# One bank for the picks' sums, three products of the features on GpSimd, and steps spread in issue order

## The chip, the cores and the metric

The program runs on one core of a Trainium2 chip. The metric is the device time of one execution in microseconds. Three executions of the kernel before took 787.77, 784.3 and 783.0 us, median 784.3. All data is float32 in memory.

## The reference

Three parts in a row. The first is a linear attention with a complex decay over 768 positions, 4 batches, 8 heads, 48 channels a head (q, k, v, a_re and a_im have the shape 4 x 8 x 768 x 48):

```
mag = sqrt(a_re^2 + a_im^2); scale = min(mag, 0.999) / (mag + 1e-6)
for t in range(768):
    (S_re, S_im) = (a_re, a_im)[t] * scale[t] * (S_re, S_im)      # complex product, per channel d
    S_re += outer(k[t], v[t])
    y[t] = q[t] @ S_re
```

Its output, 3072 tokens of 384 channels, goes through a mixture of 8 experts, one per token, chosen by an argmax (tokens with `x @ w_skip <= 0` pass unchanged): `x + gate * relu(x @ w1[e]) @ w2[e]`, with a gate from a softmax. The last part is `max(x @ m1, x @ m2, x @ m3) @ mo` with 768 inner channels.

## The kernel before

Attention runs first, the rest is a second plan that starts when its tokens are there. The recurrence is made parallel: running sums over time of the logarithm and of the angle of a turn it into products of features, and these into matrix products over chunks of 128 positions.

**Features.** A batch has three groups of 128 channel rows (`G = 3`; group g = 2 holds the channels 32 to 47 of all heads). For each group, tiles of 128 x 768: a_re and a_im (`a`), q and k (`qk`, 128 x 2 x 768), two work tiles (`CD`), and the result `R`. `ratio` (L338) takes Ln and Exp of a_re on ScalarE and multiplies by a_im on VectorE (L347), which is the ratio of the two. `stage_e` (L349) squares it on ScalarE (L352), takes more logarithms and exponentials, and scans the decay along time on VectorE (`decay`, L371). `scale` (L376) makes the reciprocal exact and multiplies `qk` with `CD` (L385, 128 x 1536). `stage_t` (L387) takes the arctangent, scans the angle (`phase`, L417), reduces it to a turn, takes sines, and makes the features by two products of 128 x 1536 (L406, L407: `R` and `qk`). `tails` copies group 2's features into the tile Y by DMAs on the SP queue. All VectorE work of a feature goes through the helper `V_` (L328; its instructions show as L332), all ScalarE work through `A_` (L300). A batch is a unit; the last batch has its group 1 cut in two parts of 4 and 2 chunks.

**Steps.** For each batch, each half of the heads (hh = 0, 1) and each chunk c of 128 positions, `step` (L459) does: transposes of k into the bank pk (L471), copied to kn by ScalarE (L473); scores of 4 heads into the 4 banks of pp (L482), copied by ScalarE to pt (L485) and masked there by GpSimd (L486; the last three steps by VectorE, L490; `POOL_MASKS` = 45 of 48); products of q with the state so far into py (L499); the state's sum z in its bank (L506), masked by VectorE into sn (L511); products of the masked scores with v into py (L519), copied by ScalarE to ysb (L521); the picks' product with w9p (L526), whose sums px lie in the upper part of py's own two banks; from there ScalarE copies the tokens to xt (L530), VectorE the router's sums to lgw (L532), and SP stores xt (L543). A step of chunk c needs the state of chunk c - 1 of its half. Banks: pk 1, pp 4, py 2, z 1: all eight. pk, pp and py exist once; pt and kn twice.

**Order.** Nothing is issued in the order written. `Plan` collects instructions with an engine, a guessed duration and the data they read and write, plays them through on these guesses (`order`), and issues each engine's instructions in the order of the planned starts. Of those that are ready it takes the one written first, shifted by a bias (`PRIO`, per batch). Each engine then runs its own list in that order on the chip and waits for data by semaphores; the guesses themselves have no further effect. Guesses are for example `t_act(n) = 93 + 0.833 n` ns for n columns on ScalarE; a rule for two-input work on GpSimd, `t_ptt(n) = 40 + 2.09 n`, stands in the file without use.

Of the kernel before, what the change touches and what calls it, by code (L numbers as in the profile page):

```python
# [166 lines left out]
NQK = 6  # L167
NR = 5
RHO0 = 2.0 ** 60
NA = 6  # L170
NPT = 2
XW = 2 * D + 9
# [13 lines left out]
def attention(tc, ctx, pl, a4, qk4, v, w9, x_dram, lg, ident, phend, rhoend, keep, early=None):  # L186
# [140 lines left out]

    def V_(name, out, *ins, n=None, bias=0, **kw):  # L328
        fn = getattr(nc.vector, name)
        t = (t_dcp if name == "tensor_scalar" else t_dve)(out[0].free_size() if n is None else n)  # L330
        names = ("in0", "in1")[:len(ins)]
        pl.add("DVE", t, lambda: fn(out=out[0], **{m: i[0] for m, i in zip(names, ins)}, **kw),  # L332
               keys(*ins), keys(out), bias=bias)

    def cut(t, n):
        return t[0][:, 0:n], t[1]

    def ratio(us):  # L338

        for u in us:  # L340
            t, k = place("CD", u)
            T[u, "C"], T[u, "D"], T[u, "CD"] = (t[:, 0, :], k), (t[:, 1, :], second(k)), (t, k + second(k))
        for w in runs(us, ("a",), "ratio"):
            A = many(w, "ar")
            A_(AF.Ln, many(w, "C"), A)
            A_(AF.Exp, A, many(w, "C"), scale=-1.0)
            V_("tensor_tensor", A, A, many(w, "ai"), op=ALU.mult, bias=PRIO["FE"][now[0]])  # L347

    def stage_e(us):  # L349
        for w in runs(us, ("a",), "log"):  # L350
            A, Dt = many(w, "ar"), many(w, "D")
            A_(AF.Square, Dt, A)  # L352
            A_(AF.Ln, Dt, Dt, bias=1.0)
        for w in runs(us, ("CD",), "size"):
            Ct, Dt = many(w, "C"), many(w, "D")
            V_("scalar_tensor_tensor", Ct, Ct, Dt, scalar=2.0, op0=ALU.mult, op1=ALU.add, bias=PRIO["FE"][now[0]])
            A_(AF.Exp, Dt, Ct, scale=0.5)
            V_("tensor_scalar", Dt, Dt, scalar1=0.999, scalar2=-1e-6, op0=ALU.min, op1=ALU.add, bias=PRIO["FE"][now[0]])
            for u in w:
                decay(u)  # L360
        for w in runs(us, ("CD",), "inv"):
            Ct, Dt = many(w, "C"), many(w, "D")
            A_(AF.Ln, Dt, Ct)
            A_(AF.Exp, Dt, Dt, scale=-1.0)

    def decay(u):
        b, g, c0, c1 = u
        Ct, Dt, i, n = T[u, "C"], T[u, "D"], b * G + g, C * (c1 - c0)

# [4 lines left out]
        pl.add("DVE", t_dve(n) + 200, scan, keys(Dt) + (("rho", i),), keys(Ct) + (("rho", i),), bias=PRIO["FE"][now[0]])  # L374
# [12 lines left out]
    def stage_t(us):  # L387
# [10 lines left out]
        for w in runs(us, ("a",), "trig"):  # L398
            A, Bt = many(w, "ar"), many(w, "ai")
            A_(AF.Abs, A, Bt)  # L400
            A_(AF.Sin, A, A, scale=-TWOPI_DOWN, bias=halfpi)
# [10 lines left out]
    def phase(u):  # L412
# [7 lines left out]
        pl.add("DVE", t_dve(n) + 200, scan, keys(A) + (("ph", i),), keys(Bt) + (("ph", i),), bias=PRIO["FT"][now[0]])  # L420

# [33 lines left out]

    prev = {}
    kfe = lambda fs: sum((f[1] for f in fs), ())

    def step(b, hh, c):  # L459
# [16 lines left out]
        pt, ptk = pl.take("pt")  # L476

        def f():
            for x, (t, _) in enumerate(fs):
                for h in range(4):  # L480
                    r = slice(ND * h, ND * h + ND)
                    nc.tensor.matmul(pp[:, h, 0:C], t[r, 1, :], t[r, 0, :], start=x == 0, stop=x == 2)  # L482
        pl.add("PE", 12 * 70, f, fk, (ppk,))
        if (2 * b + hh) * NC + c < POOL_MASKS:
            pl.add("ACT", t_acp(512), lambda: nc.scalar.copy(pt, pp[:, :, 0:C]), (ppk,), (ptk,), bias=PRIO["pt"][b])  # L485
            pl.add("POOL", 594, lambda: nc.gpsimd.affine_select(  # L486
                out=pt, in_=pt, pattern=[[0, 4], [1, C]], base=0, channel_multiplier=-1, compare_op=ALU.is_ge,
                fill=0.0), (ptk,), (ptk,))
        else:
            pl.add("DVE", t_dve(512), lambda: nc.vector.tensor_tensor(  # L490
                out=pt, in0=pp[:, :, 0:C], in1=mask[:, None, :].to_broadcast([P, 4, C]), op=ALU.mult), (ppk,), (ptk,), bias=PRIO["mask"][b])
        sp = prev.get((b, hh)) if c else None
        py, pyk = pl.take("py")
        if c:
            def f():
                for x, (t, _) in enumerate(fs):
                    for j in range(2):
                        r = slice(64 * j, 64 * j + 64)
                        nc.tensor.matmul(py[:, j, 0:C], sp[0][r, x].rearrange("p o w -> p (o w)"), t[r, 0, :], start=x == 0,  # L499
                                         stop=False, skip_group_check=True)  # L500
# [19 lines left out]
        pl.add("PE", 4 * 116, f, (vk, ptk) + ((pyk,) if c else ()), (("y", pyk),) if c else (("y", pyk), pyk))  # L520
        pl.add("ACT", t_acp(256) + 90, lambda: nc.scalar.copy(ysb, py[:, :, 0:C]), (("y", pyk), pyk), (ysk,), bias=PRIO["ysb"][b])  # L521
# [25 lines left out]
    def steps(us):  # L547
# [5 lines left out]
        for k, (b, hh) in enumerate((b, hh) for b in range(B) for hh in range(2)):  # L553
# [854 lines left out]
```

## Time and profile before

| | us |
|---|---|
| median of three executions | 784.3 |
| the profiled execution | 787.75 |
| its span | 786.0 |
| busy in the span: TensorE (PE) | 661.3 |
| VectorE (DVE) | 504.6 |
| ScalarE (ACT) | 373.2 |
| GpSimd (POOL) | 106.1 |

The profiled execution is one of its own, outside the three, and 3.45 us above their median. PE and PEld are TensorE's products and its weight loads. The span in 40 equal slices of 19.65 us; each digit is the busy share of a slice in tenths, in PEclk the granted clock in tenths of full speed:

```profile
PE   0037785877899884799999999999999999999996
DVE  6999889888751128599999975564736538313321
ACT  7597876776534323477777741232423224121221
POOL 2012012221111100211110016301202000000000
PEclk9998788597889998799999999999999999999998
```

Attention is the first 15 slices, to about 304 us; then come some 15 us of routing and first weights, and experts and the last part from 320 us on.

### The profile page before, as it was taken

What the parts mean: (1) busy time and instruction counts of PE and PEld (TensorE: products, weight loads), DVE (VectorE), ACT (ScalarE), POOL (GpSimd) and SP (SyncE); (2) the same over time, 40 slices, a digit from 0 to 9 for tenths busy, and PEclk for the clock granted to TensorE, in tenths of its full rate; (3) what the DMA queues carried; (4) which work ended last, traced back from release to release, by engine and by line L of the source; (5) the groups of instructions that cost most, each with busy time, mean ns of one, the idle gap of its engine ahead of it and who ended that gap; (6) DMA issues with size and microseconds to landing.
All of it is one profiled execution on the core that took longest, in us unless ns stands there. A gap on an engine that the chain in (4) does not pass through costs nothing.

```text
span 786.0 us, 14781 instructions
## 1 busy us (share of the span) xinstructions
PE 661.3 (84%) x5977; PEld 578.3 (74%) x5977; DVE 504.6 (64%) x828; ACT 373.2 (47%) x671; POOL 106.1 (13%) x151
## 2 busy tenths in 40 slices
PE   0037785877899884799999999999999999999996
PEld 0025664665677662699999989889789898898896
DVE  6999889888751128599999975564736538313321
ACT  7597876776534323477777741232423224121221
POOL 2012012221111100211110016301202000000000
PEclk9998788597889998799999999999999999999998
DMA  9661075411441003888888735514306031010000
GB/s 344 258 141 55 26 189 195 73 62 43 137 80 33 24 30 97 308 274 289 292 280 281 240 128 161 176 46 151 91 1 218 3 116 66 1 40 1 11 31 25
DMA packets 52108, 98.57 MB, mean 125 GB/s; under 512 B 5280, under 2 KB 41392, under 8 KB 52032
## 3 DMA queue, kind: packets, MB, share of 16 engines
q1 hardware_dynamic: 43408, 65.70, 26.8%
q10 hardware_dynamic: 5184, 20.45, 7.3%
q0 software_dynamic: 3440, 11.41, 4.8%
q8 instruction: 49, 0.80, 0.4%
q14 instruction: 27, 0.22, 0.1%
HBM read 80.23 MB, written 12.58 MB: 118 GB/s over the span
## 4 chain that ended last, share of the span: by engine, by line
PE 62%; DVE 17%; DMA 8%; issue 6%; ACT 4%; SPq 1%; POOL 0%; ACTq 0%; DVEq 0%; POOLq 0%
PE bk L838 10%; PE bk L839 10%; PE bk L840 10%; PE yb L840 5%; PE yb L839 5%; PE yb L838 5%; PE py L499 4%; PE pp L482 4%; PE py L526 3%; PE py L519 3%; DVE wa L417 2%; DMA x<-x_dram 2%; DMA wa<-in_a 2%; DVE wqk L332 2%; DVE wCD L371 2%
## 5 line engine op out<-in xcount | busy, mean ns | idle before, releaser
L838 PE MATMUL bk<-ar,wh 128*128 128x512 f32 (+1 forms) x378 | 136.4, 361 | 2.6 <-DVE xs L1117 2.0
L839 PE MATMUL bk<-ar,wh 128*128 128x512 f32 (+1 forms) x378 | 136.0, 360 | 0.1
L840 PE MATMUL bk<-ar,wl 128*128 128x512 f32 (+1 forms) x378 | 135.9, 360 | 0.0
L1117 DVE TENSOR_TENSOR xs<-bk,xs 128x512 f32<-128x512 f32 (+1 forms) x84 | 51.5, 613 | 90.8 <-PE bk L840 90.3
L838 PEld LDWEIGHTS bk<-ar,wh 128*128 128x128 f32 x378 | 71.4, 189 | 14.6 <-DVE xs L1117 3.0
L839 PEld LDWEIGHTS bk<-ar,wh 128*128 128x128 f32 x378 | 71.4, 189 | 10.6 <-DVE ar L1097 0.3
L840 PEld LDWEIGHTS bk<-ar,wl 128*128 128x128 f32 x378 | 71.4, 189 | 10.5
L486 POOL TENSOR_SCALAR_AFFINE_SELECT pt<-pt 128x512 f32<-128x512 f32 x45 | 44.5, 990 | 233.8 <-ACT pt L485 230.6
L834 DVE TENSOR_TENSOR ar<-wraw,ar 128x768 fp32r<-128x768 f32 x64 | 60.1, 953 | 5.8 <-ACT ar L833 5.2
L833 ACT CAST ar<-wraw 128x768 fp32r<-128x768 f32 x64 | 53.3, 835 | 15.1 <-PE yb L840 9.8
L838 PE MATMUL bk<-xth,ar 128*128 128x256 f32 x192 | 55.9, 291 | 1.2 <-DVE sm L935 0.7
L839 PE MATMUL bk<-xtl,ar 128*128 128x256 f32 x192 | 55.1, 287 | 0.1
L840 PE MATMUL bk<-xth,ar 128*128 128x256 f32 x192 | 54.9, 286 | 0.0
L471 PE MATMUL pk<-ident,wR 128*128 128x128 f32 x40 | 13.9, 347 | 48.7 <-DVE wR L332 48.1
L1119 ACT CAST sm<-xs 128x512 fp32r<-128x512 f32 (+1 forms) x27 | 15.1, 559 | 68.3 <-DVE xs L1117 68.3
L471 PEld LDWEIGHTS pk<-ident,wR 128*128 128x128 f32 x40 | 6.3, 157 | 53.9 <-issue 51.3
L838 PE MATMUL yb<-ar,sm 128*128 128x384 f32 x128 | 43.8, 342 | 0.0
L840 PE MATMUL yb<-ar,sm 128*128 128x384 f32 x128 | 43.1, 337 | 0.0
L839 PE MATMUL yb<-ar,sm 128*128 128x384 f32 x128 | 43.0, 336 | 0.0
L532 DVE COPY lgw<-py 128x18 f32<-128x18 f32 x48 | 8.3, 173 | 53.3 <-ACT xt L530 44.1
L300 ACT ACTIVATE wCD<-wCD 128x768 f32<-128x768 f32 (+3 forms) x51 | 39.5, 809 | 4.7 <-DVE wCD L371 4.2
L526 PE MATMUL py<-w9p,ysb 128*128 128x105 f32 x192 | 37.0, 321 | 4.7 <-ACT ysb L521 4.6
(232 smaller groups left out, 1604.0 us busy)
## 6 DMA issues: line engine op xcount, KB each, us to landing
wraw<-in_w SPq DMA_DIRECT2D x60, 384.0 KB, 4.8
wraw<-in_a ACTq DMA_DIRECT2D x12, 768.0 KB, 4.6
wqk<-in_qk SPq DMA_DIRECT2D x11, 768.0 KB, 9.0
x<-in_m ACTq DMA_DIRECT2D x9, 768.0 KB, 6.2
wa<-in_a SPq DMA_DIRECT2D x8, 768.0 KB, 5.8
v<-in_v SPq DMA_DIRECT2D x4, 1152.0 KB, 10.5
x_dram<-xt SPq DMA_DIRECT2D x48, 96.0 KB, 1.6
out<-ysb SPq DMA_DIRECT2D x24, 192.0 KB, 2.3
```

Source lines behind the costliest of these rows:

```text
L300: lambda: nc.scalar.activation(out=out[0], in_=in_[0], func=f, **kw), keys(in_), keys(out))
L482: nc.tensor.matmul(pp[:, h, 0:C], t[r, 1, :], t[r, 0, :], start=x == 0, stop=x == 2)
L486: pl.add("POOL", 594, lambda: nc.gpsimd.affine_select(out=pt, in_=pt, pattern=[[0, 4], [1, C]], base=0, channel_multiplier=-1, compare_op= ...
L499: nc.tensor.matmul(py[:, j, 0:C], sp[0][r, x].rearrange("p o w -> p (o w)"), t[r, 0, :], start=x == 0, stop=False, skip_group_check=True)
L519: nc.tensor.matmul(py[64 * o:64 * o + 64, j, 0:C], vcols(h), pt[:, h, :], start=not c, stop=True, skip_group_check=True)
L526: nc.tensor.matmul(px[:, j, :], ysb[:, j, :], w9p[:, 2 * hh + j, :], start=True, stop=True)
L833: pl.add("ACT", t_act(n), lambda: s.copy(hi, raw), r, wk_hi)
L834: pl.add("DVE", t_dve(n), lambda: v.tensor_tensor(out=lo, in0=raw, in1=f32(hi), op=ALU.subtract), tuple(r) + tuple(wk_hi), wk_lo)
L838: nc.tensor.matmul(ps, lh, rh, start=first, stop=False)
L839: nc.tensor.matmul(ps, lh, rl, start=False, stop=False)
L840: nc.tensor.matmul(ps, ll, rh, start=False, stop=last)
L1117: pl.add("DVE", t_dve(N), lambda tm=tm, ph=ph, N=N: v.tensor_tensor(out=tm[:, 0:N], in0=ph[:, 0:N], in1=tm[:, 0:N], op=ALU.max), (pk,) + t ...
```

## The change

The planner's guesses are set anew (ScalarE activations and copies, VectorE, a scan, TensorE's groups, the mask on GpSimd: 1000 ns), and `POOL_MASKS` is 48, so that all masks are GpSimd's. The picks' sums px get a bank of their own; for it pk goes, and the three transposes of k are written to columns 128 to 255 of three of the score banks, in the same group of TensorE work as the scores. kn is copied from there, and pt and kn have three buffers each. Three products of each group run on GpSimd: the ratio (128 x 768), the square (128 x 768, before ScalarE's) and qk with CD (128 x 1536). `pace` adds to the planner's list, for a batch but the last, a predecessor on VectorE for the k-th of its 12 score groups, such that the groups are spread over 95% of the planned VectorE work from this batch's first step to the next one's. These predecessors are used by the planner alone.

```diff
-t_act = lambda n: 93 + 0.833 * n
-t_acp = lambda n: 51 + 0.833 * n
-t_dve = lambda n: 70 + 1.04 * n
+t_act = lambda n: 150 + 0.85 * n
+t_acp = lambda n: 160 + 0.833 * n
+t_dve = lambda n: 90 + 1.04 * n
+t_scan = lambda n: 330 + 2.15 * n
-POOL_MASKS = 45
+POOL_MASKS = 48
+PACE = 0.95
+SIDE = {(w, b, g) for w in ("ratio", "scale", "square") for b in range(B) for g in range(G)}
-NPT = 2
+NPT = 3
-    ring("kn", [P, 3, P], 2)
+    ring("kn", [P, 3, P], 3)
-    ring("pk", [P, 512], 1, psum)
+    ring("px", [P, 512], 1, psum)
+    work = set()
...
-    def V_(name, out, *ins, n=None, bias=0, **kw):
-        fn = getattr(nc.vector, name)
+    def V_(name, out, *ins, bias=0, eng="DVE", **kw):
+        fn = getattr(nc.gpsimd if eng == "POOL" else nc.vector, name)
...
+        if eng == "DVE":
+            work.add(len(pl.ops))
+    def side(what, u):
+
+        return "POOL" if (what, u[0], u[1]) in SIDE else "DVE"
...
-            V_("tensor_tensor", A, A, many(w, "ai"), op=ALU.mult, bias=PRIO["FE"][now[0]])
+            V_("tensor_tensor", A, A, many(w, "ai"), op=ALU.mult, bias=PRIO["FE"][now[0]], eng=side("ratio", w[0]))
...
-            A_(AF.Square, Dt, A)
+            if side("square", w[0]) == "POOL":
+                V_("tensor_tensor", Dt, A, A, op=ALU.mult, eng="POOL")
+            else:
+                A_(AF.Square, Dt, A)
...
-                V_("tensor_tensor", T[u, "qk"], T[u, "qk"], T[u, "CD"], op=ALU.mult, bias=PRIO["scale"][now[0]])
+                V_("tensor_tensor", T[u, "qk"], T[u, "qk"], T[u, "CD"], op=ALU.mult, bias=PRIO["scale"][now[0]], eng=side("scale", u))
...
-        if not last:
-            pk, pkk = pl.take("pk")
-            kn, knk = pl.take("kn")
-
-            def f():
-                for x, (t, _) in enumerate(fs):
-                    nc.tensor.transpose(pk[:, x * P:x * P + P], t[:, 1, :], ident)
-            pl.add("PE", 3 * 97, f, fk, (pkk,))
-            pl.add("ACT", t_acp(384), lambda: nc.scalar.copy(kn.rearrange("p x r -> p (x r)"), pk[:, 0:3 * P]), (pkk,), (knk,),
-                   bias=PRIO["kn"][b])
...
-        pl.add("PE", 12 * 70, f, fk, (ppk,))
+            if not last:
+                for x, (t, _) in enumerate(fs):
+                    nc.tensor.transpose(pp[:, 1 + x, C:C + P], t[:, 1, :], ident)
+        gates_.setdefault(b, []).append(pl.add("PE", 880 if last else 1220, f, fk, (ppk,)))
...
+        if not last:
+            kn, knk = pl.take("kn")
+            pl.add("ACT", t_acp(384), lambda: nc.scalar.copy(kn, pp[:, 1:4, C:C + P]), (ppk,), (knk,), bias=PRIO["kn"][b])
...
-        px = py[:, :, C:C + XW]
+        px, pxk = pl.take("px")
+        px = px[:, 0:2 * XW].rearrange("p (j w) -> p j w", j=2)
...
-        pl.add("PE", 2 * 218, f, (ysk, "w9p"), (("px", pyk),))
+        pl.add("PE", 2 * 218, f, (ysk, "w9p"), (pxk,))
...
+            ends.setdefault(b, len(pl.ops))
             step(b, hh, c)
+
+    def pace():
+
+        dve = [i for i, o in enumerate(pl.ops) if o[0] == "DVE" and i in work]
+        for b in range(B - 1):
+            span = [i for i in dve if ends[b] <= i < ends[b + 1]]
+            total = sum(pl.ops[i][1] for i in span)
+            at, k = 0, 0
+            for i in span:
+                while k < len(gates_[b]) and at >= total * PACE * k / len(gates_[b]):
+                    if k and at:
+                        pl.ops[gates_[b][k]][3].setdefault(last_, False)
+                    k += 1
+                at += pl.ops[i][1]
+                last_ = i
```

## Rows read from the trace of the kernel before

**Rows 1.** Busy times by stretch: us, then PE, PEld, DVE, ACT, POOL, clock, DMA.
```profile
55.00:216.00 161.00, 122.34 (x1862) 95.79 (x1854) 137.92 (x181) 113.45 (x204) 32.42 (x28) 0.80 0.35 100
226.50:304.00 77.50, 68.59 (x1263) 53.99 (x1263) 20.51 (x62) 26.95 (x69) 10.15 (x16) 1.00 0.12 31
```

**Rows 2.** Timeline of VectorE, its ends: start us, us, instruction, [idle before].
```profile
225.78 0.68 DVE L332 TENSOR_TENSOR wqk<-wqk,wa 128x512 f32<-128x512 f32 x1
...
303.64 0.18 DVE L532 COPY lgw<-py 128x18 f32<-128x18 f32 x1
```

**Rows 3.** Groups by line of VectorE, 55 to 216 us: count, busy, mean ns, idle.
```profile
L511 DVE TENSOR_TENSOR sn<-zst,odd 128x288 f32<-128x288 f32 x24 | 10.9, 453 | 7.9 <-PE py L499 7.9
...
L532 DVE COPY lgw<-py 128x18 f32<-128x18 f32 x25 | 4.2, 170 | 13.2 <-PE py L526 9.0 <-ACT xt L530 4.2
```

**Rows 4.** Timeline of TensorE, products with v in the tail.
```profile
246.78 0.66 PE L519 MATMUL py<-pt,v 128*64 128x128 f32 x8
...
250.61 0.66 PE L519 MATMUL py<-pt,v 128*64 128x128 f32 x8
...
257.40 0.66 PE L519 MATMUL py<-pt,v 128*64 128x128 f32 x8
...
301.43 0.66 PE L519 MATMUL py<-pt,v 128*64 128x128 f32 x8
```

**Rows 5.** Timeline of VectorE, undisturbed: 768 and 1536 columns.
```profile
24.78 0.95 DVE L332 SCALAR_TENSOR_TENSOR wR<-wCD 128x768 f32<-128x768 f32 x1
25.65 1.75 DVE L332 TENSOR_TENSOR wqk<-wqk,wCD 128x1536 f32<-128x1536 f32 x1
```

**Rows 6.** Selects on GpSimd beside no features: a group, and one in the timeline.
```profile
L237 POOL TENSOR_SCALAR_AFFINE_SELECT mask<-mask 128x128 f32<-128x128 f32 x1 | 0.3, 292 | 0.0
...
244.59 0.63 POOL L486 TENSOR_SCALAR_AFFINE_SELECT pt<-pt 128x512 f32<-128x512 f32 x1 [2.86 <-ACT pt L485]
```

**Rows 7.** Timelines of VectorE and GpSimd, where a select meets a feature.
```profile
129.74 1.75 DVE L417 TENSOR_TENSOR_SCAN wa<-wa,zero 128x768 f32<-128x768 f32 x1
129.84 2.08 POOL L486 TENSOR_SCALAR_AFFINE_SELECT pt<-pt 128x512 f32<-128x512 f32 x1 [4.86 <-ACT pt L485]
...
181.29 0.63 POOL L486 TENSOR_SCALAR_AFFINE_SELECT pt<-pt 128x512 f32<-128x512 f32 x1 [6.06 <-ACT pt L485]
181.31 1.15 DVE L332 SCALAR_TENSOR_TENSOR wR<-wCD 128x512 f32<-128x512 f32 x1
182.50 0.69 DVE L332 SCALAR_TENSOR_TENSOR wCD<-wR,wCD 128x512 f32<-128x512 f32 x1
```

**Rows 8.** Groups by line: 1536-wide products without selects (20 to 55), with them, and selects.
```profile
L332 DVE TENSOR_TENSOR wR<-wqk,wa 128x1536 f32<-128x1536 f32 x3 | 5.3, 1751 | 0.0
L332 DVE TENSOR_TENSOR wqk<-wqk,wCD 128x1536 f32<-128x1536 f32 x3 | 5.3, 1750 | 0.0
L332 DVE TENSOR_TENSOR wqk<-wqk,wa 128x1536 f32<-128x1536 f32 x2 | 3.5, 1751 | 0.0
...
L332 DVE TENSOR_TENSOR wR<-wqk,wa 128x1536 f32<-128x1536 f32 x8 | 14.8, 1848 | 0.0
L332 DVE TENSOR_TENSOR wqk<-wqk,wCD 128x1536 f32<-128x1536 f32 x8 | 14.6, 1829 | 0.0
L332 DVE TENSOR_TENSOR wqk<-wqk,wa 128x1536 f32<-128x1536 f32 x8 | 14.3, 1788 | 0.0
...
L486 POOL TENSOR_SCALAR_AFFINE_SELECT pt<-pt 128x512 f32<-128x512 f32 x28 | 33.8, 1206 | 176.5 <-ACT pt L485 176.5
```

**Rows 9.** Groups by line of attention, 0 to 304 us: idle before, and releasers.
```profile
L482 PE MATMUL pp<-wR 32*128 32x128 f32 x384 | 27.3, 358 | 8.5 <-ACT pt L485 8.3
...
L499 PE MATMUL py<-wR,sn 64*128 64x128 f32 x160 | 22.8, 367 | 15.7 <-DVE lgw L532 12.4 <-ACT xt L530 3.3
...
L473 ACT COPY kn<-pk 128x384 f32<-128x384 f32 x40 | 19.3, 482 | 5.7 <-PE pk L471 2.7 <-PE zst L506 2.3
```

**Rows 10.** Timeline of the SP queue: four stores of a step.
```profile
74.46 21.12 SPq L543 DMA_DIRECT2D x_dram<-xt  x4
```

More of the change, by code (lines that the diff above doesn't have):

```diff
@@ L326, in keys @@
         return sum((t[1] for t in ts), ())
-    def V_(name, out, *ins, n=None, bias=0, **kw):
-        fn = getattr(nc.vector, name)
-        t = (t_dcp if name == "tensor_scalar" else t_dve)(out[0].free_size() if n is None else n)
+    def V_(name, out, *ins, bias=0, eng="DVE", **kw):
+        fn = getattr(nc.gpsimd if eng == "POOL" else nc.vector, name)
+        t = ((t_pts if name == "tensor_scalar" else t_ptt) if eng == "POOL" else t_dcp if name == "tensor_scalar" else t_dve)(out[0].free_size())
         names = ("in0", "in1")[:len(ins)]
-        pl.add("DVE", t, lambda: fn(out=out[0], **{m: i[0] for m, i in zip(names, ins)}, **kw),
+        if eng == "DVE":
+            work.add(len(pl.ops))
+        pl.add(eng, t, lambda: fn(out=out[0], **{m: i[0] for m, i in zip(names, ins)}, **kw),
                keys(*ins), keys(out), bias=bias)
@@ L373, in scan @@
             nc.vector.tensor_copy(out=rhoend[:, i:i + 1], in_=Ct[0][:, n - 1:n])
-        pl.add("DVE", t_dve(n) + 200, scan, keys(Dt) + (("rho", i),), keys(Ct) + (("rho", i),), bias=PRIO["FE"][now[0]])
+        work.add(len(pl.ops))
+        pl.add("DVE", t_scan(n), scan, keys(Dt) + (("rho", i),), keys(Ct) + (("rho", i),), bias=PRIO["FE"][now[0]])
     def scale(us):
@@ L399, in stage_t @@
             A, Bt = many(w, "ar"), many(w, "ai")
-            A_(AF.Abs, A, Bt)
+            if side("abs", w[0]) == "POOL":
+                V_("scalar_tensor_tensor", A, Bt, Bt, scalar=-1.0, op0=ALU.mult, op1=ALU.max, eng="POOL")
+            else:
+                A_(AF.Abs, A, Bt)
             A_(AF.Sin, A, A, scale=-TWOPI_DOWN, bias=halfpi)
@@ L419, in scan @@
             nc.vector.tensor_copy(out=phend[:, i, c0:c1], in_=c3(Bt[0])[:, :, C - 1])
-        pl.add("DVE", t_dve(n) + 200, scan, keys(A) + (("ph", i),), keys(Bt) + (("ph", i),), bias=PRIO["FT"][now[0]])
+        work.add(len(pl.ops))
+        pl.add("DVE", t_scan(n), scan, keys(A) + (("ph", i),), keys(Bt) + (("ph", i),), bias=PRIO["FT"][now[0]])
     def tails(u):
@@ L454, in feats @@
         return out
-    prev = {}
+    prev, gates_, ends = {}, {}, {}
     kfe = lambda fs: sum((f[1] for f in fs), ())
@@ L482, in f @@
                     nc.tensor.matmul(pp[:, h, 0:C], t[r, 1, :], t[r, 0, :], start=x == 0, stop=x == 2)
-        pl.add("PE", 12 * 70, f, fk, (ppk,))
+            if not last:
+                for x, (t, _) in enumerate(fs):
+                    nc.tensor.transpose(pp[:, 1 + x, C:C + P], t[:, 1, :], ident)
+        gates_.setdefault(b, []).append(pl.add("PE", 880 if last else 1220, f, fk, (ppk,)))
         if (2 * b + hh) * NC + c < POOL_MASKS:
             pl.add("ACT", t_acp(512), lambda: nc.scalar.copy(pt, pp[:, :, 0:C]), (ppk,), (ptk,), bias=PRIO["pt"][b])
-            pl.add("POOL", 594, lambda: nc.gpsimd.affine_select(
+            pl.add("POOL", 1000, lambda: nc.gpsimd.affine_select(
                 out=pt, in_=pt, pattern=[[0, 4], [1, C]], base=0, channel_multiplier=-1, compare_op=ALU.is_ge,
@@ L500, in f @@
                                          stop=False, skip_group_check=True)
-            pl.add("PE", 6 * 130, f, fk + (sp[1],), (pyk,))
+            pl.add("PE", 870, f, fk + (sp[1],), (pyk,))
         if not last:
@@ L507, in f @@
                                          start=c == 0 and x == 0, stop=c == NC - 2 and x == 2, skip_group_check=True)
-            pl.add("PE", 12 * 37, f, (vk, knk), ("z",) + (("begun",) if (b, hh, c) == (B - 1, 1, 0) else ()))
+            pl.add("PE", 390, f, (vk, knk), ("z",) + (("begun",) if (b, hh, c) == (B - 1, 1, 0) else ()))
             sn, snk = pl.take("sn")
@@ L520, in step @@
         pl.add("PE", 4 * 116, f, (vk, ptk) + ((pyk,) if c else ()), (("y", pyk),) if c else (("y", pyk), pyk))
-        pl.add("ACT", t_acp(256) + 90, lambda: nc.scalar.copy(ysb, py[:, :, 0:C]), (("y", pyk), pyk), (ysk,), bias=PRIO["ysb"][b])
-        px = py[:, :, C:C + XW]
+        pl.add("ACT", t_acp(256), lambda: nc.scalar.copy(ysb, py[:, :, 0:C]), (("y", pyk), pyk), (ysk,), bias=PRIO["ysb"][b])
+        px, pxk = pl.take("px")
+        px = px[:, 0:2 * XW].rearrange("p (j w) -> p j w", j=2)
         def f():
@@ L526, in f @@
                 nc.tensor.matmul(px[:, j, :], ysb[:, j, :], w9p[:, 2 * hh + j, :], start=True, stop=True)
-        pl.add("PE", 2 * 218, f, (ysk, "w9p"), (("px", pyk),))
+        pl.add("PE", 2 * 218, f, (ysk, "w9p"), (pxk,))
         xt, xtk = pl.take("xt")
         t0 = (b * NC + c) * C
-        pl.add("ACT", t_acp(192) + 90, lambda: nc.scalar.copy(xt.rearrange("p (j o) e -> p j (o e)", o=2), px[:, :, 0:2 * D]),
-               (("px", pyk), pyk), (xtk,), bias=PRIO["xt"][b])
+        pl.add("ACT", t_acp(192), lambda: nc.scalar.copy(xt.rearrange("p (j o) e -> p j (o e)", o=2), px[:, :, 0:2 * D]),
+               (pxk,), (xtk,), bias=PRIO["xt"][b])
         pl.add("DVE", 150, lambda: nc.vector.tensor_copy(out=lgw[:, (b * NC + c) % (2 * NC), 2 * hh:2 * hh + 2, :],
                                                          in_=px[:, :, 2 * D:]),
-               (("px", pyk), pyk), (("lgw", b % 2, c, hh),), bias=PRIO["lgw"][b])
+               (pxk,), (("lgw", b % 2, c, hh),), bias=PRIO["lgw"][b])
         sums = {NC - 1: 0} if b < B - 1 else {NC - 1 - LAST: 0, NC - 1: NC - LAST}
@@ L576, in attention @@
             stage_t(us)
+    pace()
     if early:
```

## The prediction

> **What bounds the kernel now.** I looked first at busy times by stretch, because a mean over the span mixes an attention stage with an expert stage that the change does not touch. From 55 to 216 us [rows 1] VectorE is busy 138 of 161 us while TensorE is busy 122 at a granted clock of 0.80; from 226.5 to 304 us VectorE is busy 21 of 77.5, and TensorE 69 at 1.00. So one stretch belongs to VectorE, the next to TensorE. Then the instructions in order of time [rows 2]: the last feature instruction of the last batch ends on VectorE at 226.5, the last instruction of the last attention step at 303.8. Call these F and E. Behind E come routing and experts, which wait for attention; I take them as shifted and otherwise unchanged. The change is worth what it moves E.
>
> Why 77 us between F and E? The groups by line [rows 3] count 25 finished steps by 216; two more end by F. So 21 of 48 steps are left: the 12 of the last batch, which could hardly come earlier, and 9 of the batch before, which could. The reader should see a backlog here: TensorE had been able to make a step only every 161/25 = 6.4 us while the features ran, against 3.83 us once they are gone (two successive products with v, [rows 4]). Twelve steps cost 11 x 3.83 from the first such product to the last, and 2.4 from there to the end [rows 2, 4], 44.5 us; in this kernel the same twelve took 46.4.
>
> **The change, part by part.**
>
> *Products to GpSimd: VectorE's relief.* Per group of features one 768-wide and one 1536-wide product leave VectorE. From start to start such instructions take 0.87 and 1.67 us [rows 5] (the printed time is 0.08 longer, an overlap). Twelve groups: 12 x 2.54 = 30.5 us. ScalarE loses a square per group; it is busy 113 of 161 us [rows 1], not the bound, so I count nothing for that.
>
> *The price on GpSimd.* No product of two tiles runs there before. The nearest rows are selects: 0.29 us for 128 columns, 0.63 for 512 [rows 6], so 0.9 ns a column and 0.18 fixed. Lower end: a product costs like a select, 0.86 and 1.54 us, 2 x 0.86 + 1.54 = 3.3 per group, 39 in all. Upper end: each of its two inputs costs what the select's one does, 1.55 and 2.92, 6.0 per group, 72 in all. I take the upper one, since two tiles have to be read. The Trainium skill, page "GPSIMD Engine Reference", section "Elementwise — side-by-side cycle accounting", measures 4497 ns for 2048 columns; as an estimate from that page 1.7 and 3.4 us, 81 in all, and the sum below would end 5 us later. No run here shows it.
>
> *What these 72 us take back from VectorE.* The rows show the engines holding each other up. A select that starts at 129.84, just after a scan, needs 2.08 us instead of 0.63 and ends after the scan; an instruction of 512 columns that starts at 181.31, just after a select, needs 1.15 us where its twin needs 0.69 [rows 7]: 0.46 of the select's 0.63 us is lost to VectorE. Leaving out 0.17 fixed per instruction, the products hold VectorE for up to 66 us. How much of that hits? Lower end: the three groups of 1536-wide products [rows 8] lost 8 x (97 + 79 + 37) ns = 1.7 of 42 us, 4.1%, while 28 selects of 0.63 us covered 11% of the stretch, a share of 0.37. Upper end: all of it, VectorE always having something to run. I take 0.65, 43 us, above the middle of what the selects did, since a product is up to five times as long as a select and fits no pause.
>
> The Trainium skill, page "SBUF — State Buffer", section "Who interferes with whom", speaks against the change: a VectorE instruction with two SBUF inputs and a GpSimd instruction that reads SBUF contend for one shared port, and whichever comes second waits the other out entirely. By that rule the share is near 1 and the change is the slower rival below; the trace agrees on single pairs (the 2.08 and 1.15 us) and not on the mean (0.37).
>
> *Picks' sums in their own bank.* The next step's products into py no longer wait until the sums of this one have been copied out. Before, TensorE's first product into py sat idle 15.7 us in all behind these copies [rows 9], and lgw's copy stands in VectorE's queue behind features. This goes; the state product (sn), also in VectorE's queue, is late next.
>
> *Transposes of k in the score banks.* Three transposes move into the score group, with nothing added on TensorE; but the next scores now wait for kn's copy too, 0.48 us behind or ahead of pt's. They waited 8.3 us for pt before [rows 9]; 40 x 0.48 = 19 us is the most that comes on top, nothing the least. I set it against the 15.7 removed, both to nothing: TensorE idled 39 of 161 us there. In the tail the scores' own loop is shorter than a step and hides it. The third pt and kn buffers and three more masks on GpSimd instead of VectorE are hidden there as well: TensorE is the bound at the end.
>
> *Steps spread.* Pace adds entries to the planner's list only; no instruction waits for more data. What moves is the order on TensorE and, with each step, its mask on GpSimd, its copies on ScalarE and VectorE and its store on SP. SP is in order: four stores in a row held it for 21 us [rows 10], with loads behind them; spread stores may do better or worse by a few us, and I take none. On GpSimd a mask may now stand behind a 2.9 us product, and TensorE's queue behind that mask. Nine steps more before F add 9 x 0.46 = 4 us of sn and lgw to VectorE (0.453 and 0.170 less the overlap twice, [rows 3]). TensorE must make 36 steps between 55 and the new F, 5.2 us each; I let one be late, 3.8 us.
>
> **The sum.** F: 226.5 - 30.5 + 43 + 4 = 243. E: 243 + 3.8 + 44.5 = 291.3, 12.5 us earlier than 303.8. The profiled execution took 787.75 us (span 786.0), 3.45 above the median of 784.3; taken off the median, 771.8: **772 us**. Ends of the unknowns: share 0.37 puts it 19 us lower, share 1 adds 23, the lower price takes off 21.
>
> **Rivals.** (a) *The products are nearly free*: share 0.37 of the upper price (24 us), or the lower price (some 21). F is then about 221 to 224, TensorE becomes the bound and a few steps stay late: E near 274, **754 us**. For it: the mean of the selects. Against: their shortness.
>
> (b) *GpSimd becomes the bound* (slower). Every microsecond of a product stands VectorE still: F = 226.5 - 30.5 + 66 + 4 = 266, E = 310.5, **791**; with the masks queued between products and every product waiting for a VectorE instruction before it, some 10 us of idle more, **801**. It decides from a loss of 55.5 us, a share of 0.84, at which E is where it was. For it: the single pairs [rows 7]. Against: 23 of 161 us in which VectorE ran nothing, and sn and lgw, which read PSUM.
>
> (c) *The backlog stays* (slower, or hardly different). If a step still needs 6.4 us while features run, since sn waits in VectorE's queue and masks in GpSimd's, (243 - 55)/6.4 = 29 steps are done, 7 late ones add 27 us: E = 314.5, **795**. The spread that does nothing to the real order is this with 9 late: **802**. For it: sn and lgw waits that the order alone cannot mend. Against: the bank of their own.
>
> **How the numbers follow.** A measurement here tells about 1%, 7.8 us, from no change: below 776.5 is faster, above 792.1 slower. The forecast gets 0.38 (758 to 784: 0.30 of it faster, 0.08 within 1%), (a) 0.25, all faster, (b) 0.17, (c) 0.15 (0.06 within, 0.09 slower); 0.05 remain for small effects that cancel, within 1%. Faster 0.55, within 0.19, slower 0.26. The range reaches from (a) with both low ends, 742, to (b) and (c) at 803.
>
> **What would show it.** Right: the last feature instruction on VectorE near 243, 12 or 13 steps left there, the picks' sums never waited for, products of some 1.6 and 2.9 us on GpSimd, VectorE's scans longer than 1.75 beside them. (a): scans unchanged, F before 225, TensorE busy throughout. (b): F past 262, scans and products waiting for GpSimd. (c): over 15 steps left at F. It would be wrong altogether if the expert stage moved by itself.

## The result, and the profile after

The changed kernel takes **795.15 us** (median of four executions, 794.04 to 796.91) against 784.27 for the kernel before in the same comparison: ratio 1.0131, 95% interval 1.0092 to 1.017. 772 was forecast. Of views by group and by wait selected lines are shown, one below the other; in timelines three dots mark what is left out. The profiled execution took 794.67 us, its span is 793.0. Three rows of the page's 40 slices (19.8 us each) show the attention stage and the experts behind it:

```profile
PE   0006878749588994789999999999999999999996
DVE  5996985896699328689999975573735538313321
POOL 8516846382672111211120016300202000000000
```

GpSimd, at 0 to 2 tenths before, is at 3 to 8 in nine of the first eleven slices; VectorE's digits are lower in five of the first eleven slices, and stay high for about two slices longer. Next the busy times by stretch, with the columns of [rows 1], first of the kernel after, then (up to its own last feature) of the kernel before:

```profile
55.00:216.00 161.00, 117.92 (x1838) 93.28 (x1842) 123.53 (x137) 104.16 (x185) 91.08 (x52) 0.83 0.40 112
0.00:261.00 261.00, 157.01 (x2484) 124.28 (x2486) 211.40 (x239) 158.65 (x273) 143.20 (x135) 0.87 0.41 122
```

```profile
0.00:226.50 226.50, 135.54 (x2040) 105.77 (x2040) 194.47 (x253) 156.21 (x261) 39.84 (x90) 0.84 0.46 137
```

From 55 to 216 us every engine but GpSimd does less than before: VectorE 124 us instead of 138, TensorE 118 instead of 122. VectorE is worse off in two ways: it is busy for 211.4 us instead of 194.5 up to the last feature, though 30.5 us of work left it (its instructions stand still while a product runs, as shown below; this lost time is called the standstill here), and it idles, between instructions, 261.0 - 211.4 = 49.6 us instead of 32.0. The timeline gives the ends that answer to [rows 2], and the first product of the experts:

```profile
260.26 0.69 DVE L338 TENSOR_TENSOR wqk<-wqk,wa 128x512 f32<-128x512 f32 x1
...
307.07 0.16 DVE L547 COPY lgw<-px 128x18 f32<-128x18 f32 x1
...
323.14 0.58 PE L870 MATMUL bk<-xth,ar 128*128 128x256 f32 x1 [0.30 <-ACT xth L933]
```

So F = 261.0 (243 forecast) and E = 307.2 (291.3 forecast, 303.8 before). By F 35 steps are finished, 13 are left. The groups by line up to 315 us show the products and what stands beside them (mean ns of one after the busy time, then idle before and its releasers):

```profile
L338 POOL TENSOR_TENSOR wqk<-wqk,wCD 128x1536 f32<-128x1536 f32 x11 | 47.2, 4293 | 16.4 <-DVE wCD L338 16.4
L338 POOL TENSOR_TENSOR wa<-wa 128x768 f32<-128x768 f32 x11 | 22.8, 2084 | 21.6 <-ACT wa L304 21.6
L338 POOL TENSOR_TENSOR wCD<-wa 128x768 f32<-128x768 f32 x9 | 15.1, 1694 | 0.1
L434 DVE TENSOR_TENSOR_SCAN wa<-wa,zero 128x768 f32<-128x768 f32 x11 | 24.5, 2228 | 0.0
L338 DVE SCALAR_TENSOR_TENSOR wCD<-wR,wCD 128x768 f32<-128x768 f32 x11 | 23.0, 2101 | 0.1
L525 DVE TENSOR_TENSOR sn<-zst,odd 128x288 f32<-128x288 f32 x40 | 18.1, 452 | 23.0 <-PE zst L520 22.9
L436 DVE COPY phend<-wa 128x6 f32<-128x6 f32 x11 | 13.1, 1192 | 0.4
L513 PE MATMUL py<-wR,sn 64*128 64x128 f32 x160 | 21.7, 351 | 1.7 <-ACT wa L304 1.7
L520 PE MATMUL zst<-v,kn 128*32 128x48 f32 x960 | 21.3, 230 | 29.3 <-ACT kn L505 20.0 <-DVE sn L525 8.2 <-DVE wa L735 0.5
```

A 1536-wide product takes 4.29 us on GpSimd, 2.92 were counted; on VectorE it took 1.67 from start to start [rows 5]. The wait behind the picks' sums, 15.7 us in [rows 9], is gone from the products into py (L513), as forecast; 2.9 us of waiting for lgw's copy stand before the picks' own product now (L541), whose bank that copy has to empty. Once the features have begun to come, TensorE waits most for kn's copy (20.0 us). How a VectorE instruction of 0.95 us [rows 5] becomes one of 4.07, the timeline of both engines shows:

```profile
27.52 0.95 DVE L338 SCALAR_TENSOR_TENSOR wR<-wCD 128x768 f32<-128x768 f32 x1
27.68 4.07 POOL L338 TENSOR_TENSOR wqk<-wqk,wCD 128x1536 f32<-128x1536 f32 x1 [8.46 <-DVE wCD L338]
28.50 4.07 DVE L338 SCALAR_TENSOR_TENSOR wCD<-wR,wCD 128x768 f32<-128x768 f32 x1
...
37.45 1.75 DVE L434 TENSOR_TENSOR_SCAN wa<-wa,zero 128x768 f32<-128x768 f32 x1
37.61 4.80 POOL L338 TENSOR_TENSOR wqk<-wqk,wCD 128x1536 f32<-128x1536 f32 x1 [0.89 <-DVE wCD L338]
39.23 3.20 DVE L436 COPY phend<-wa 128x6 f32<-128x6 f32 x1
```

The first product ends at 31.75. The instruction beside it starts at 28.50 and ends at 32.57, 0.82 us later: it ran when the product was over. It goes the other way too: this product starts at 27.68, while a VectorE instruction runs until 28.47, and of its 4.07 us 3.28 come after that. The product that starts 0.16 us after the start of a scan takes 4.80 us, 3.21 of them after the scan's end, and a copy of six columns beside it takes 3.20. The Trainium skill, page "SBUF — State Buffer", section "Who interferes with whom", says that of a VectorE instruction with two SBUF inputs and a GpSimd instruction that reads SBUF one waits for the other as a whole; these rows agree, and so does sn, which reads one of its two inputs from PSUM and takes 452 ns here as before [rows 3].

### The profile page after: what moved, and what is told of

It is laid out like the page before. It is cut to its first block, busy times and chain, and to the rows that moved or that the text cites. A ratio compares the mean times of both kernels' runs of the same rounds, so it can differ in the third digit from the quotient of the medians.

```text
span 793.0 us, 14833 instructions
## 1 busy us (share of the span) xinstructions
PE 657.0 (83%) x5977; PEld 577.2 (73%) x5977; DVE 516.5 (65%) x799; ACT 368.3 (46%) x662; POOL 206.5 (26%) x192
## 4 chain that ended last, share of the span: by engine, by line
PE 57%; DVE 16%; issue 9%; DMA 7%; ACT 7%; POOL 2%; SPq 0%; ACTq 0%; DVEq 0%; POOLq 0%
PE bk L870 9%; PE bk L872 9%; PE bk L871 9%; PE yb L871 4%; PE yb L872 4%; PE yb L870 4%; PE pp L490 4%; PE px L541 3%; DVE wa L434 3%; DVE wCD L338 2%; PE py L533 2%; DMA x<-x_dram 2%; PE py L513 2%; PE pp L493 2%; PE zst L520 2%
## 5 line engine op out<-in xcount | busy, mean ns | idle before, releaser
L870 PEld LDWEIGHTS bk<-ar,wh 128*128 128x128 f32 x378 | 71.4, 189 | 15.3 <-DVE xs L1149 3.3
L497 POOL TENSOR_SCALAR_AFFINE_SELECT pt<-pt 128x512 f32<-128x512 f32 x48 | 48.3, 1008 | 113.7 <-ACT pt L496 113.7
L490 PE MATMUL pp<-wR 32*128 32x128 f32 x384 | 27.3, 358 | 56.0 <-DVE wR L338 56.0
L490 PEld LDWEIGHTS pp<-wR 32*128 32x128 f32 x384 | 17.1, 209 | 62.6 <-DVE wR L338 56.0
L338 POOL TENSOR_TENSOR wqk<-wqk,wCD 128x1536 f32<-128x1536 f32 (+2 forms) x13 | 52.5, 4038 | 16.4 <-DVE wCD L338 16.4
L520 PE MATMUL zst<-v,kn 128*32 128x48 f32 x960 | 21.3, 230 | 29.3 <-ACT kn L505 20.0
L541 PE MATMUL px<-w9p,ysb 128*128 128x105 f32 x192 | 35.0, 309 | 12.1 <-ACT ysb L535 9.2
L870 PE MATMUL yb<-ar,sm 128*128 128x384 f32 x128 | 43.4, 339 | 0.0
L915 POOL DMA_INDIRECT xs<-x_dram,r_tok x16 | 19.6, 1225 | 89.7 <-PE bk L927 75.4
```

Of the source, the lines that this page charges most:

```text
L338: pl.add(eng, t, lambda: fn(out=out[0], **{m: i[0] for m, i in zip(names, ins)}, **kw), keys(*ins), keys(out), bias=bias)
L497: pl.add("POOL", 1000, lambda: nc.gpsimd.affine_select(out=pt, in_=pt, pattern=[[0, 4], [1, C]], base=0, channel_multiplier=-1, compare_op ...
L870: nc.tensor.matmul(ps, lh, rh, start=first, stop=False)
```

## The experiments

All ratios are to the kernel before, run beside each kernel; its own medians there lie between 783.9 and 785.8 us, so that times of different experiments compare to about 2 us. F, E and X (start of the experts' first product) are read from the timeline of the one profiled execution of each kernel, VectorE's busy time from the busy times up to F, idle is the rest of the time up to F; "steps" counts lgw's copies up to F.

| kernel | median us | F | busy | idle | steps | E | X | span |
|---|---|---|---|---|---|---|---|---|
| before | 784.3 | 226.5 | 194.5 | 32.0 | 27 | 303.8 | 320.6 | 786.0 |
| after | 795.15 | 261.0 | 211.4 | 49.6 | 35 | 307.2 | 323.1 | 793.0 |
| e1_noside | 754.1 | 212.4 | 197.1 | 15.3 | 33 | 265.8 | 282.7 | 751.8 |
| e2_sideonly | 820.5 | 256.2 | 206.8 | 49.4 | 27 | 327.7 | 351.2 | 816.9 |
| e3_nopace | 800.1 | 255.0 | 208.6 | 46.4 | 36 | 305.3 | 324.9 | 798.2 |
| e4_banks | 757.8 | 219.0 | 198.2 | 20.8 | 36 | 269.1 | 285.5 | 755.8 |
| e5_xread | 815.2 | 274.1 | 255.6 | 18.5 | 32 | 329.9 | 346.6 | 815.3 |
| e6_xwrite | 766.6 | 222.9 | 207.3 | 15.6 | 32 | 277.2 | 293.1 | 764.2 |
| e7_scale | 786.0 | 249.6 | 216.5 | 33.1 | 36 | 294.5 | 310.9 | 785.1 |
| e8_square | 768.5 | 229.5 | 205.6 | 23.9 | 34 | 280.8 | 297.4 | 769.1 |
| e9_oldexp | 753.2 | 212.2 | 197.4 | 14.8 | 33 | 265.6 | 282.1 | 748.4 |
| e10_guess | 790.4 | 221.1 | 195.7 | 25.4 | 27 | 300.7 | 317.5 | 788.1 |
| e11_bankonly | 749.6 | 215.7 | 198.7 | 17.0 | 34 | 262.5 | 281.3 | 746.8 |
| e12_guess2 | 798.8 | 264.3 | 211.1 | 53.2 | 36 | 306.8 | 326.4 | 795.6 |

**The products taken back.**

```diff
-SIDE = {(w, b, g) for w in ("ratio", "scale", "square") for b in range(B) for g in range(G)}
+SIDE = set()
```

> The changed kernel with the three products back on VectorE and ScalarE (SIDE empty), all else kept. Theory A, GpSimd's products stand VectorE still for their whole length: the last feature instruction, at 261 us in the changed kernel, comes 45 to 50 us of standstill earlier and 30 us of returned work later, near 243; and as the backlog of steps stays away, attention ends near 288 and the time is 770 to 780 us. Theory B, the spread order and the moved transposes cost the time: it stays at 790 to 797.

754.13 us, ratio 0.9638 (0.9572 to 0.9705): all the rest of the change is worth 30 us, and the products cost 795.15 - 754.13 = 41. That is faster than theory A's 770 to 780, which had only the standstill go and left VectorE's idle time as it was; the idle time falls from 49.6 us to 15.3. Its busy times and VectorE's waits (total us, times, longest) up to F:

```profile
0.00:212.40 212.40, 133.32 (x2359) 105.39 (x2363) 197.06 (x262) 162.46 (x278) 43.48 (x95) 0.94 0.51 150
```

```profile
DVE lgw L547 <- PE px L541: 2.9, 4, 1.7
DVE wCD L338 <- ACT wCD L304: 2.2, 3, 1.1
DVE sn L525 <- PE zst L520: 0.7, 1, 0.7
```

**The products alone**, in the kernel before:

```diff
...
+    def V_(name, out, *ins, n=None, bias=0, eng="DVE", **kw):
+        fn = getattr(nc.gpsimd if eng == "POOL" else nc.vector, name)
...
+            V_("tensor_tensor", A, A, many(w, "ai"), op=ALU.mult, bias=PRIO["FE"][now[0]], eng=side("ratio", w[0]))
...
+                V_("tensor_tensor", Dt, A, A, op=ALU.mult, eng="POOL")
...
+                V_("tensor_tensor", T[u, "qk"], T[u, "qk"], T[u, "CD"], op=ALU.mult, bias=PRIO["scale"][now[0]], eng=side("scale", u))
```

> The kernel before with the three products on GpSimd and nothing else of the change. Theory A: the features end 20 to 35 us later than at 226.5, part of the backlog is worked off meanwhile; 795 to 810 us. Theory B: as before or faster, 775 to 787.

820.48 us, ratio 1.048 (1.0417 to 1.0544). VectorE's 206.8 us are 194.5 - 30.5 + 42.8 at the same 27 steps, and its idle grows from 32.0 to 49.4. The two costs of the products, the standstill and the idle time, are there without the other parts of the change. The time lies above theory A's 795 to 810, since no part of the backlog was worked off by F: 27 steps, as before. From 55 to 216 us TensorE is left with the least work of all the kernels, and the lowest clock:

```profile
55.00:216.00 161.00, 104.36 (x1597) 80.99 (x1601) 130.60 (x140) 103.87 (x180) 81.63 (x48) 0.75 0.34 91
```

**No pace**, with the products and without:

```diff
-    pace()
```

> The changed kernel without pace, products still on GpSimd. Theory A: the products still cost the same; if pace is what removed the backlog, 9 steps are left again and it is 10 to 25 us slower than the changed kernel (805 to 820); if the bank of the picks' sums did, 793 to 798. Theory B: 780 to 787.

800.1 us, ratio 1.0213 (1.015 to 1.0275), nearer to the 793 to 798 expected if the bank removed the backlog than to the 805 to 820 if pace did.

```diff
-SIDE = {(w, b, g) for w in ("ratio", "scale", "square") for b in range(B) for g in range(G)}
+SIDE = set()
...
-    pace()
```

> The changed kernel with neither the products on GpSimd nor pace: the banks, the third buffers, the three masks and the planner's guesses alone. Theory A: no standstill; 760 to 784, and its distance to the kernel with pace but without the products is what pace is worth. Theory B, if the moved transposes cost time (the next scores wait for kn too): 787 or more.

757.78 us, ratio 0.9673 (0.9601 to 0.9745), 2 us under the range of theory A. Pace brings 5 us with the products and 4 without, each time with overlapping intervals; 36 steps are done by F in both. It isn't pace that removes the backlog.

**Reading or writing?** The kernel without the products, and beside its features work of the same places and sizes on tiles that nobody else uses: products that read, or fills that only write. One call of 768 columns stands in ratio, one behind the square and one of 1536 in scale, 13 of each, as the last batch's group 1 comes in two parts.

```diff
...
+    def extra(n, r):
+        pl.add("POOL", t_ptt(n), lambda: nc.gpsimd.tensor_tensor(out=sb_[:, 0:n], in0=sa_[:, 0:n], in1=sa_[:, 0:n], op=ALU.mult), keys(r), ("sb",))
...
+                extra(768, T[u, "ar"])
...
+                extra(1536, T[u, "D"])
```

> The changed kernel with the products back on VectorE and ScalarE, and beside them, per group, two products of 768 columns and one of 1536 on GpSimd that read and write scratch tiles only: no instruction of the kernel uses their result, so only what they hold up can cost. Theory A, GpSimd's reading stands VectorE's two-input instructions still: VectorE keeps its 30 us of products and loses 40 to 50 us besides; the features end at 250 to 262 us instead of 212 and the time is 790 to 805 us. Theory C, the changed kernel lost its time because features waited for slow products and ScalarE and VectorE stood in the chain: nobody waits here, 754 to 762.

815.19 us, ratio 1.0376 (1.0333 to 1.0418), 10 us above theory A's range. Its busy times up to F:

```profile
0.00:274.10 274.10, 154.29 (x2297) 123.51 (x2301) 255.62 (x260) 163.80 (x275) 148.16 (x135) 0.83 0.40 116
```

```diff
...
+        pl.add("POOL", t_ptt(n), lambda: [nc.gpsimd.memset(sb_[:, 0:m], 0.0) for m in ((1536, 1536, 768) if n > 768 else (1536,))], keys(r), ("sb",))
```

> The same with fills of a scratch tile in place of these products, about as long on GpSimd (3840 columns for the 1536-wide product, 1536 for a 768-wide one), that read nothing. Theory A (reading is what collides): VectorE's scans and products keep their 1.75 us, 754 to 765 us, the rest for masks that stand behind a fill. Theory D, GpSimd's queue is the trouble, masks and steps waiting behind long instructions: the same as with the scratch products, 785 or more.

766.62 us, ratio 0.9798 (0.9744 to 0.9851), 2 us above theory A's range and far from theory D's. Groups of the products' kernel, then of the fills', then of e1:

```profile
L352 POOL TENSOR_TENSOR sb<-sa 128x768 f32<-128x768 f32 x26 | 56.9, 2189 | 1.2
L352 POOL TENSOR_TENSOR sb<-sa 128x1536 f32<-128x1536 f32 x13 | 46.2, 3551 | 0.3
L394 DVE TENSOR_TENSOR_SCAN wCD<-wCD,zero 128x768 f32<-128x768 f32 x11 | 27.0, 2459 | 0.1
```

```profile
L352 POOL MEMSET sb<- 128x1536 f32 x52 | 73.8, 1420 | 1.9
L352 POOL MEMSET sb<- 128x768 f32 x13 | 10.2, 784 | 0.8
L394 DVE TENSOR_TENSOR_SCAN wCD<-wCD,zero 128x768 f32<-128x768 f32 x11 | 19.8, 1803 | 0.1
L341 DVE TENSOR_SCALAR wa<-wa 128x768 int32<-128x768 f32 x11 | 11.0, 1032 | 0.0
L447 DVE COPY phend<-wa 128x6 f32<-128x6 f32 x11 | 7.6, 692 | 0.4
```

```profile
L384 DVE TENSOR_TENSOR_SCAN wCD<-wCD,zero 128x768 f32<-128x768 f32 x11 | 19.5, 1770 | 0.1
L338 DVE TENSOR_SCALAR wa<-wa 128x768 int32<-128x768 f32 x11 | 5.7, 549 | 0.0
L436 DVE COPY phend<-wa 128x6 f32<-128x6 f32 x11 | 2.4, 216 | 0.4
```

103 us of products that nobody waits for cost 61 us against e1, 84 us of fills 12.5. With the products VectorE's instructions grow by 58.5 us (255.6 against 197.1) and its idle by 3. So most of the burden doesn't come from GpSimd or its queue being occupied, for masks stand behind fills as well; it comes from what GpSimd reads. The same Trainium skill section excepts work that only writes from that collision, and the scan's 1.80 us beside the fills against 2.46 beside the products agrees. The fills are not free all the same: VectorE's instructions grow by 10.2 us beside them (207.3 against 197.1), and what grows there are instructions with one input, the 768-wide ones with an int32 result from 549 to 1032 ns and the copies of six columns from 216 to 692.

**One product at a time.**

```diff
+SIDE = {(w, b, g) for w in ("scale",) for b in range(B) for g in range(G)}
```

> The changed kernel with only the 1536-wide product (qk with CD) on GpSimd. Theory A: each holds VectorE 4.1 us and saves it 1.67: 12 x 2.4 = 29 us at most, 772 to 783 us. Theory C: 754 to 765.

```diff
+SIDE = {(w, b, g) for w in ("square",) for b in range(B) for g in range(G)}
```

> The changed kernel with only the square on GpSimd, which relieves ScalarE and not VectorE. Theory A: 12 x 1.5 us of standstill and no relief for VectorE, 8 to 18 us: 762 to 772. Theory C, a shorter ScalarE queue helps: 750 to 754.

scale alone: 786.0 us, ratio 1.0005 (0.998 to 1.003), 32 us above e1 and 3 above theory A's range, which counted no idle time; square alone, which relieves ScalarE and not VectorE: 768.49, 0.9771 (0.9719 to 0.9824), 14 above. For scale VectorE's busy time is 216.5 = 197.1 - 12 x 1.67 + 3 x 0.46 (three more steps) + 38.0: each product saved 1.67 us there and held the engine up for 3.2. Besides, the idle grows by 17.8 us for scale and 8.6 for the square. The ratio alone was not run; the two costs that were, 32 and 14 us, already add up to more than the 41 of all three, so they are not simply additive.

**The guesses.** Without the products (`SIDE` empty), the old guesses for the experts' plan; and the kernel before with the new guesses for ScalarE, VectorE and the scan and nothing else:

```diff
...
+            globals().update(t_act=lambda n: 93 + 0.833 * n, t_acp=lambda n: 51 + 0.833 * n, t_dve=lambda n: 70 + 1.04 * n)
             with ExitStack() as c2:
```

> The changed kernel with the products back on VectorE and ScalarE, and with the old planner's guesses for ScalarE and VectorE put back for the second plan, that of the experts. In the kernel before, the time from the experts' first product to the end was 465.4 us, in the changed kernel 469.9, without its products 469.1. Theory E, the new guesses change the experts' order for the worse: 465 to 466 us here, and 749 to 752 us in all. Theory F, the stage varies from run to run: 468 to 471, 753 to 755.

```diff
+t_act = lambda n: 150 + 0.85 * n
+t_acp = lambda n: 160 + 0.833 * n
+t_dve = lambda n: 90 + 1.04 * n
+t_scan = lambda n: 330 + 2.15 * n
...
```

> The kernel before with the new guesses for ScalarE, VectorE and the scan and nothing else. Theory E: experts 468 to 471 us. If the guesses also mend the attention order, its last step ends before 300 us and the time is under 781; if the bank did, 784 to 792.

e9: 753.24 us, 0.9595 (0.956 to 0.9631), not told apart from e1. e10: 790.38 us, 1.0086 (1.0056 to 1.0116): these guesses alone make the kernel slower by some 6 us, though in the profiled execution attention ends 3 us earlier. F comes 5.4 us earlier, with 27 steps done by it as before, so they don't mend the backlog. They order the experts too. From X to the end of the span the plans with old guesses take 465.4 to 466.3 us (before, e2, e9, e11), the ten with the new ones 468.7 to 474.2 (e10: 470.7). By this stage theory E holds, though e9's time in all is the one that theory F expected.

**The bank alone**, with the move of the transposes that makes room for it: no products, no pace, two buffers of pt and kn, 45 masks, and the guesses of the kernel before, but for those of TensorE's groups, of GpSimd's mask (1000 ns instead of 594) and of the copies to ysb and xt (90 ns less). What these few guesses do to the order was not run apart.

```diff
...
+SIDE = set()
+NPT = 2
+POOL_MASKS = 45
+    ring("kn", [P, 3, P], 2)
+t_act = lambda n: 93 + 0.833 * n
+t_acp = lambda n: 51 + 0.833 * n
+t_dve = lambda n: 70 + 1.04 * n
+t_scan = lambda n: 270 + 1.04 * n
-    pace()
```

> The kernel before with the banks exchanged and nothing else of the change but the durations of TensorE's groups in a step: old guesses, two buffers for pt and kn, 45 masks on GpSimd, no pace, no products there. If the picks' bank removed the backlog, the features end near 220 us with 13 to 16 steps left and the time is 755 to 768; if the third buffers and the guesses did, 775 to 787. Theory E: experts 465 to 466 us.

**749.63 us**, ratio 0.9558 (0.9516 to 0.96), the best of all, faster than both kernels and 5 us under the range expected if the bank removed the backlog. Busy times from 55 to 216 us, and VectorE's waits up to F:

```profile
55.00:216.00 161.00, 135.01 (x2424) 109.38 (x2425) 149.91 (x202) 122.81 (x234) 38.84 (x36) 0.96 0.42 111
```

```profile
DVE sn L525 <- PE zst L520: 6.2, 7, 1.8
DVE lgw L547 <- PE px L541: 1.6, 3, 0.7
```

Against [rows 1] TensorE does 135 us of work instead of 122 in that stretch, at a mean granted clock of 0.96 of full speed (2.4 GHz) instead of 0.80, and VectorE 150 instead of 138. 34 steps are done by F instead of 27, so F to E is 46.8 us instead of 77.3.

**Is the idle a matter of the order?** The changed kernel with guesses set to what its own trace measured:

```diff
-t_scan = lambda n: 330 + 2.15 * n
+t_scan = lambda n: 380 + 2.25 * n
-t_ptt = lambda n: 40 + 2.09 * n
+t_ptt = lambda n: 40 + 2.75 * n
-        t = ((t_pts if name == "tensor_scalar" else t_ptt) if eng == "POOL" else t_dcp if name == "tensor_scalar" else t_dve)(out[0].free_size())
+        t = ((t_pts if name == "tensor_scalar" else t_ptt) if eng == "POOL" else t_dcp if name == "tensor_scalar" else lambda n: 1.27 * t_dve(n))(out[0].free_size())
```

> The changed kernel, with the first plan's guesses set to what its trace measured: a product on GpSimd 40 + 2.75 n ns instead of 40 + 2.09 n (4264 for 1536 columns), VectorE's two-input work 1.27 times its guess (the 211.4 us it took against 167 without the standstill), a scan 2108 ns instead of 1981. No instruction is added or taken away; only the order of issue may differ. Theory G (the order is planned too tight: VectorE's 34 us of additional idle up to the last feature come from steps placed where TensorE is not ready yet, because the plan doesn't know the standstill): the idle falls from 49.6 towards 20, the last feature comes near 235 instead of 261, and the median is near 772. Rival S (the idle comes with any order, because the true dependencies now run through GpSimd): the idle stays near 50, the last feature near 260, the median within 6 us of 795.

798.78 us, ratio 1.0197 (1.0149 to 1.0244). Up to F:

```profile
0.00:264.30 264.30, 161.31 (x2550) 127.29 (x2551) 211.10 (x242) 160.99 (x277) 138.44 (x136) 0.91 0.41 122
```

```profile
DVE lgw L547 <- ACT xt L545: 16.6, 12, 2.6
DVE wCD L338 <- ACT wCD L304: 15.2, 8, 8.1
DVE sn L525 <- PE zst L520: 13.4, 8, 3.2
```

Theory G falls, S holds: the idle is 53.2 us, spread over other waits. A plan with these longer durations doesn't avoid it.

## Why the prediction was wrong

**How long VectorE is busy was forecast right, by luck.** 194.5 - 30.5 + 43 + 4 = 211.0 us of instructions up to F by the prediction's terms, 211.4 measured. The standstill worked out the same way is 211.4 - 194.5 + 30.5 - 8 x 0.46 = 43.7. The two factors behind it were both off and cancelled: the products take 98 us on GpSimd in all instead of 72 (groups above and their smaller forms), so that 0.45 of their time is lost on VectorE, not 0.65 of 66. A part of the 98 us, 0.8 and 1.6 us of the two products in the timeline, is GpSimd standing for VectorE, which the prediction had no term for. The Trainium skill, page "GPSIMD Engine Reference", section "Elementwise — side-by-side cycle accounting" (4497 ns for 2048 columns, 3.4 us for 1536 as an estimate), was nearer than the prediction's upper end from selects: 3.55 us on tiles that nobody else uses, 4.29 on the real ones. (Its 81 us less the fixed part, times 0.65, would have put the prediction's sum 6 us later, not 5.)

**The step that failed: "F: 226.5 - 30.5 + 43 + 4".** Adding terms to 226.5 carries VectorE's 32.0 us of idle over unchanged. It became 49.6: 211.4 + 49.6 = 261.0, and those 17.6 us are F's whole miss of 18 but for 0.4. Against the kernel without the products the difference is 34.3 us. The waits up to F show it:

```profile
DVE lgw L547 <- PE px L541: 15.5, 11, 2.2
DVE sn L525 <- PE zst L520: 15.0, 12, 3.7
DVE wCD L338 <- ACT wCD L304: 9.1, 5, 6.7
```

2.9, 0.7 and 2.2 in e1: these three grew by 33.8 us (smaller ones cancel). VectorE, in order, stands before a step's sn or lgw that TensorE hasn't made ready, and before ScalarE's logarithms and exponentials, which now wait for products from GpSimd. That this comes from the products being links of the chain, not from the standstill, is what e5 and e8 show. e5 has more standstill (58.5 us) from products that nobody waits for, and only 3 us more idle; e8, in which VectorE keeps all its own products as in e5, has 8.6 us more idle from the square alone, at 8.5 us more of busy time. TensorE's clock doesn't decide it either: up to F it is granted 0.83 in e5, with 18.5 us of idle, and 0.91 in e12, with 53.2. The idle grows with each real product that was tried alone (17.8 us for scale), and e12's longer guesses don't remove it. Which of the chain's links costs how much of the 34 us was not separated.

**The rival that came true is (b)**, though not as it was put: it had the standstill at 66 us and 10 of idle at its upper end; the runs show 44 and 17.6. Its mark, F past 262, was missed by one us, its 791 and 801 enclose the result, and with 0.17 its chance was too low. (Its E, 266 + 44.5, leaves out the 3.8 us of a late step that the forecast and the decision point count; with them it would be 795 and 805.) The decision point, a loss of 55.5 us, was right in kind: 43.7 + 17.6 = 61.3 us were lost, 5.8 more, and E came 3.4 later than before.

**The bank exchange "both to nothing"** is the other large mistake; only its sign relative to the products hid it. Without the products, pace and most of the new guesses (e11) it is worth 784.3 - 749.6 = 35 us. The prediction put the 15.7 us that py waited against up to 19 us of waiting for kn. It should have asked whose queue the wait held up. VectorE's waits up to F in the kernel before:

```profile
DVE sn L511 <- PE py L499: 9.4, 9, 1.5
DVE lgw L532 <- PE py L526: 9.0, 5, 2.7
DVE lgw L532 <- ACT xt L530: 4.6, 3, 2.1
```

In e11 lgw's 13.6 us become 3.3 and sn's 9.4 become 6.2; VectorE's idle falls from 32.0 to 17.0, so F comes 11 us earlier with seven more steps done, and F to E is 30.5 us shorter. Beside the products VectorE's idle stays at 49.6 (49.4 in e2), so that on F nothing of this is left; the shorter tail remains.

**Right: the backlog.** Rival (c) did not happen, though its 795 us is the time measured: its mark was over 15 steps left at F, and 13 are left as forecast, and F to E takes 46.2 us instead of 77.3 (48.3 forecast). But the reason is the bank, not the spread: e2, without the bank, has 27 steps by F as before, e4 and e11, with it and without pace, have 36 and 34.

**"Shifted and otherwise unchanged" (routing and experts)** missed by 3.6 us: 482.2 from E to the end of the span before, 485.8 after, of which 4.5 from X on. e9 and e10 show the cause to be the guesses, which order the experts' plan as well.

The sum of the misses: E +15.9, behind E +3.6, and 3.9 since the profiled execution was 3.45 above its median before and is 0.5 below it after: 23.4, for 795.15 - 771.8 = 23.3.

## What to carry to other kernels

Before work goes from VectorE to GpSimd, set what it saves there (1.67 us) against what it holds up there (3.2 us): with reading work on both sides the sum was negative here, though GpSimd had time to spare (busy 97.7 of 249.6 us up to F in e7). A sum that adds terms to an engine's end time carries its idle over; where a moved instruction becomes a link between engines that each run their own list in order, give the idle a term and bounds of its own. And time the parts of a change apart: here one part alone made the kernel 4.4% faster, and another alone 4.8% slower.

## What the runs showed of the hardware that was not expected

- A VectorE copy of six columns took 3.20 us beside a 1536-wide product on GpSimd (1.19 on average in the changed kernel, 0.216 in e1). Beside fills it still took 0.69 on average, while scans hardly slowed (1.80 against 1.77).
- Between 55 and 216 us the granted clock is mostly higher where TensorE has more to do: 1597 products at 0.75 of full speed (e2), 1862 at 0.80 (before), 1838 at 0.83 (after), 2424 at 0.96 (e11). On TensorE e11 differs from the kernel before only in the place of the transposes and of the picks' sums, and in the order. Which of the two drives the other no run here separates.
